# First two blocks of four sequence pairs moved to the front, and the weight pieces re-placed, in a windowed-attention and MLP kernel

## The chip, the cores and the metric

The kernel runs on one core of a Trainium2 chip. The metric is the device time of one execution in microseconds (us). TensorE is called PE below, ScalarE ACT, VectorE DVE, GpSimd POOL and SyncE SP.

## The reference

Eight sequences of 576 tokens, eight heads of 64, in float32. Attention with a causal window of 128 tokens and a linear distance bias, then a layer norm, a two-layer MLP (512 to 2048 to 512) and a residual:

```python
scores = scale * np.matmul(q, k.transpose(0, 1, 3, 2))
rel = pos[:, None] - pos[None, :]
bias = slopes[:, None, None] * (-np.abs(rel))[None, :, :]
mask = (rel >= 0) & (rel < window)          # window = 128
scores = np.where(mask, scores + bias[None], -1e9)
attn = softmax(scores); x = np.matmul(attn, v)   # laid out as [B, S, 512]
xn = (x - mu) / np.sqrt(var + 1e-06) * g_ln
out = x + np.maximum(xn @ w_ch1, 0.0) @ w_ch2
```

## The kernel before, in words

The 8 x 576 tokens are 36 blocks of 128. Two sequences make a pair of nine blocks; block 4 of a pair holds the end of one sequence and the start of the next. Within its pair a block has a number r from 0 to 8. A block with r = 0 looks only at itself, every other one also at the block before it.

Each block goes through `attention(i)` (L545): q and k are brought in, cast to 16 bits and turned so that the head dimension lies on partitions (`qkt`); then bias matmuls Z (L741; only in the first BY_BIAS blocks, later ones multiply with a mask table on DVE instead, L780), score matmuls S (L725), an exponential on ACT (L773), probability-value matmuls pv (L797), normalisation on DVE (L814, L818), centring xs (L858) and a transpose of xs on PE (TX, L872) whose copy is xt. Chunks of 3, 2, 3 and then 4 blocks go through `mlp(c)` (L907): layer 1, 16 groups of four matmuls (L919) with a relu on ACT or DVE, and layer 2 (L947) with the residual on DVE (L955). The eight weight pieces w0 to w7 (four of each layer, 1 MB in float32 each) are cast while POOL's DMA queue brings them in (L536, L538).

There are three ways for q and k. In a *span*, SP loads two neighbouring blocks as token pairs (`load_span`, L455: 512-byte packets, tiles `qs` and `ks`), one cast on POOL, DVE or ACT interleaves them (L619, L621), and PE turns both blocks together as 32-bit pairs (L639). A single block below LOAD_CAST comes by SP in 256-byte packets (`load`, L359), is cast (L560) and turned on PE (L687). From LOAD_CAST on, POOL's queue casts on the way (L473), and from QK_BY_DMA on a DMA transpose turns the block. The v of the first five blocks comes by SP and is cast to `vx` on ACT or POOL (L591, L593); later v comes by POOL's queue. Block 4 of the first pair is a single block in halves: six transfers of 64 partitions.

All of this is recorded as tasks. A planner (`Plan.run`, L103) plays them through with a cost for each engine, deadlines (`av`), hand-set shifts (PRI, HOLD) and lists of engines allowed for a cast or copy (PICK); it models DMA queues with rates (L96). The order in which it starts tasks is then written out for each engine (L988), with idle matmuls on a zero tile (L986) where PE has nothing to do in the first WARM microseconds of the plan. Waits on the chip come only from data and buffers: a dependency that exists in the plan alone, such as "weight piece n after the v cast of block i" (`weights`, L528, with W_AFTER, L525), orders instructions only where both stand on the same engine.

```python
    W_AFTER = [6, 12, 17, 18, 21, 22, 22, 28]
...
        if i in span_of:
            weights(i, (third,) * 3)
```

An entry of W_AFTER is three times a block's place plus 0, 1 or 2 for its q, k or v; in a span block all three stand for the v (`third`, L600).

Of the kernel before, what the change touches and what calls it, by code (L numbers as in the profile page):

```python
# [26 lines left out]
class Ring:  # L27
    def __init__(self, tiles):
        self.tiles, self.first, self.readers = tiles, {}, {}

    def __getitem__(self, k):
        return self.tiles[k % len(self.tiles)]
# [7 lines left out]
    def link(self):  # L40
        n = len(self.tiles)
        for k, tasks in self.first.items():
            for t in tasks:
                t.deps += self.readers.get(k - n, [])


class Plan:
# [8 lines left out]
    LANDING = {"DMA SP": (0.7, 1.3), "DMA ACT": (0.7, 1.3), "DMA POOL": (2.1, 1.4)}  # L56
    LAST_OF_RUN = 1.0
# [6 lines left out]
    def ring(self, tiles):  # L64
        r = Ring(tiles)
        self.rings.append(r)
        return r
# [28 lines left out]
    def rates(self, queues):  # L96
        on = [q for q, x in queues.items() if x]
        if "DMA POOL" in on and len(on) > 1:
            a, b = (0.92, 0.17) if len(queues["DMA POOL"]) > 1 else (0.7, 0.4)
            return {q: a if q == "DMA POOL" else b / (len(on) - 1) for q in on}  # L100
        return {q: 1.0 / len(on) for q in on}
# [125 lines left out]
def kernel(  # L227
# [10 lines left out]
    nc = tc.nc  # L238
# [30 lines left out]
    WARM = 22.0  # L269
    TABLE_AFTER = 4  # L270
    STATS_LEAD = 10.0
    MIX_AFTER = 4
    SPLIT = 4
    LOAD_CAST = 9
    V_CAST = 5
    BY_HALVES = [0, 2, 5]
    HALVED = []
    SPANS = [0, 2, 5, 7]
    SLACK = (0, 0.2, 0)
    PICK = {('xt', 0): 'ACT', ('xt', 8): 'ACT DVE', ('cv', 5): 'ACT', ('cv', 0): 'POOL', ('ev', 8): 'ACT', ('ev', 1): 'DVE ACT', ('ev', 3): 'ACT', ('ck', 8): 'ACT', ('cq', 5): 'ACT', ('ev', 5): 'DVE', ('ck', 2): 'POOL', ('ck', 7): 'POOL ACT', ('cq', 6): 'POOL', ('cq', 2): 'POOL ACT', ('xt', 6): 'ACT', ('cq', 8): 'POOL', ('xt', 5): 'ACT', ('cv', 7): 'POOL ACT', ('cv', 3): 'ACT', ('xt', 3): 'DVE', ('ev00', 4): 'ACT', ('cs1', 1): 'POOL ACT', ('cs0', 0): 'POOL DVE', ('ev10', 3): 'ACT', ('xt', 2): 'DVE', ('cq', 3): 'POOL', ('cs0', 8): 'ACT', ('ev01', 8): 'DVE ACT', ('ev10', 8): 'DVE ACT', ('ev11', 5): 'ACT', ('cs0', 2): 'DVE', ('cq', 4): 'POOL', ('ev00', 8): 'DVE', ('ev01', 0): 'DVE ACT', ('cv', 8): 'POOL ACT', ('ev11', 0): 'ACT', ('cv', 4): 'POOL ACT', ('ev01', 6): 'ACT', ('cv', 6): 'POOL ACT', ('ev10', 5): 'ACT', ('cs1', 4): 'POOL', ('ev', 0): 'DVE', ('cv', 2): 'POOL ACT', ('ev00', 2): 'DVE ACT', ('ev00', 7): 'ACT', ('ev10', 2): 'ACT', ('xt', 1): 'ACT DVE', ('ev11', 8): 'DVE', ('xt', 4): 'DVE', ('ev00', 1): 'DVE ACT', ('cv', 1): 'POOL ACT', ('ev01', 7): 'DVE ACT', ('ev11', 6): 'DVE ACT', ('cq', 1): 'ACT', ('ev01', 4): 'DVE', ('cs0', 5): 'POOL', ('ev', 7): 'ACT', ('xt', 7): 'ACT DVE', ('ev', 9): 'ACT', ('cv', 9): 'POOL', ('cq', 11): 'POOL ACT', ('cs1', 9): 'POOL ACT', ('ev00', 10): 'ACT', ('eva', 5): 'ACT', ('cka', 9): 'ACT', ('cv', 11): 'POOL ACT', ('cqa', 10): 'DVE', ('ckb', 10): 'ACT', ('ck', 10): 'ACT', ('ev00', 5): 'ACT', ('ckb', 3): 'DVE', ('evb', 5): 'DVE', ('ev', 11): 'DVE', ('ev01', 2): 'DVE ACT', ('ckb', 6): 'ACT', ('eva', 11): 'DVE', ('cqb', 7): 'POOL DVE ACT', ('cka', 1): 'POOL DVE ACT', ('ev00', 3): 'ACT', ('cq', 0): 'ACT', ('ev01', 5): 'DVE', ('cqb', 5): 'DVE', ('ev10', 4): 'DVE ACT', ('ev01', 9): 'ACT', ('cqa', 8): 'ACT', ('ev10', 10): 'DVE', ('evb', 4): 'DVE ACT', ('cqb', 8): 'POOL ACT', ('cs0', 9): 'POOL DVE', ('cka', 3): 'POOL', ('cqa', 2): 'DVE', ('cka', 8): 'ACT', ('cqa', 5): 'POOL DVE ACT', ('cq', 7): 'POOL', ('ck', 1): 'POOL', ('cka', 0): 'POOL ACT', ('cqa', 7): 'ACT', ('ev10', 11): 'ACT', ('cqa', 4): 'ACT', ('ev11', 11): 'DVE', ('eva', 10): 'DVE ACT', ('ev11', 4): 'DVE', ('eva', 3): 'DVE', ('ev11', 2): 'DVE', ('cqa', 6): 'POOL', ('cqa', 9): 'POOL ACT', ('cqa', 11): 'POOL DVE ACT', ('ev', 2): 'DVE ACT', ('cs0', 4): 'POOL ACT', ('ckb', 11): 'DVE', ('ckb', 2): 'POOL DVE ACT', ('ck', 5): 'POOL', ('cs1', 8): 'ACT', ('ev01', 10): 'DVE ACT', ('ev', 10): 'DVE ACT', ('cq', 10): 'POOL', ('eva', 4): 'DVE', ('cv', 10): 'POOL', ('ev', 6): 'DVE ACT', ('ck', 11): 'ACT', ('cs1', 11): 'POOL ACT', ('cqb', 1): 'DVE', ('ckb', 7): 'DVE', ('ev11', 1): 'DVE ACT', ('ck', 4): 'POOL ACT', ('cka', 11): 'DVE', ('ckb', 0): 'POOL ACT', ('cs1', 0): 'POOL DVE', ('eva', 7): 'DVE', ('cs0', 11): 'POOL ACT', ('evb', 8): 'DVE ACT', ('ev10', 6): 'DVE', ('eva', 2): 'DVE', ('cqb', 2): 'ACT', ('cq', 9): 'POOL ACT', ('ev10', 9): 'DVE ACT', ('ev10', 0): 'DVE ACT', ('evb', 6): 'DVE ACT', ('eva', 8): 'ACT', ('cqa', 3): 'POOL ACT', ('ck', 9): 'ACT', ('evb', 3): 'DVE ACT', ('cs0', 1): 'DVE', ('cqb', 9): 'POOL DVE ACT', ('cqb', 0): 'POOL', ('evb', 2): 'ACT', ('evb', 1): 'ACT', ('cqb', 6): 'DVE', ('eva', 9): 'ACT', ('evb', 10): 'ACT', ('cqb', 11): 'DVE', ('cka', 10): 'POOL', ('ck', 6): 'POOL ACT', ('ckb', 1): 'POOL', ('ev10', 7): 'ACT', ('cs1', 7): 'ACT', ('ev01', 3): 'DVE', ('cs0', 7): 'POOL', ('cs0', 6): 'POOL DVE', ('cs1', 3): 'DVE', ('cka', 2): 'POOL ACT', ('cqa', 1): 'POOL ACT', ('ev01', 1): 'ACT', ('cs0', 10): 'POOL ACT', ('cka', 4): 'ACT', ('ev00', 6): 'DVE', ('xt', 10): 'DVE', ('cqb', 3): 'POOL DVE ACT', ('evb', 0): 'DVE ACT', ('ev00', 0): 'ACT', ('xt', 9): 'ACT', ('ev11', 7): 'DVE', ('cqb', 4): 'POOL DVE ACT', ('ev00', 9): 'DVE', ('ev00', 11): 'DVE ACT', ('ckb', 9): 'POOL ACT', ('ev11', 3): 'DVE ACT', ('ev01', 11): 'DVE', ('evb', 7): 'DVE ACT', ('ckb', 4): 'POOL ACT', ('ckb', 5): 'POOL ACT', ('cs1', 5): 'ACT', ('cs0', 3): 'POOL DVE', ('cka', 7): 'POOL', ('ev11', 9): 'DVE', ('cka', 5): 'ACT', ('cqb', 10): 'POOL', ('cs1', 6): 'POOL DVE', ('eva', 6): 'DVE', ('cs1', 10): 'POOL ACT', ('eva', 1): 'DVE', ('evb', 9): 'DVE ACT', ('ev10', 1): 'ACT', ('eva', 0): 'DVE', ('cka', 6): 'POOL ACT', ('ev11', 10): 'ACT', ('ev', 4): 'ACT', ('ck', 3): 'POOL ACT', ('cs00', 0): 'POOL ACT', ('cs10', 3): 'DVE', ('cs01', 10): 'ACT', ('cs11', 6): 'POOL', ('cs00', 9): 'POOL', ('cs01', 11): 'POOL', ('cs11', 9): 'ACT', ('cs00', 6): 'POOL DVE', ('cs11', 3): 'POOL DVE', ('cs01', 7): 'POOL', ('cs01', 8): 'POOL DVE', ('cs10', 11): 'POOL ACT', ('cs00', 8): 'DVE', ('cqa', 0): 'ACT', ('cs00', 2): 'POOL', ('cs01', 6): 'DVE', ('cs10', 4): 'DVE', ('cs10', 10): 'POOL ACT', ('cs00', 4): 'POOL', ('ck', 0): 'ACT', ('cs11', 5): 'DVE', ('cs11', 2): 'POOL', ('cs11', 8): 'DVE', ('cs01', 1): 'POOL', ('cs01', 4): 'POOL DVE', ('cs00', 1): 'POOL DVE', ('cs11', 0): 'POOL', ('ckb', 8): 'DVE', ('cs10', 9): 'POOL ACT', ('cs01', 9): 'POOL ACT', ('cs00', 10): 'POOL', ('cs01', 2): 'POOL', ('cs00', 5): 'POOL', ('cs11', 11): 'ACT', ('cs00', 3): 'POOL ACT', ('cs10', 1): 'ACT', ('cs01', 3): 'POOL', ('cs11', 1): 'DVE', ('cs11', 10): 'POOL DVE', ('cs11', 4): 'ACT', ('cs10', 6): 'POOL ACT', ('cs11', 7): 'ACT', ('cs10', 0): 'DVE', ('cs10', 5): 'ACT', ('cs10', 7): 'POOL'}  # L280
    PRI = {'T7.1': -4.2, 'A1.13': 6.1, 'rc0.8': -3.5, 'B4.0': 5.4}
    HOLD = {'mkb5': 43.12, 'v8.i': 46.02, 'nm0.7': 54.13, 'cT0.01': 7.07, 'cT5.10': 33.76, 'qs0.0.i': 1.25, 'g.i': 0.8, 'sid1': 4.85, 'mreg00': 28.48, 'z1': 31.56, 'r0.3': 28.11, 'r0.11': 36.69, 'rc1.8': 61.94}
    BY_BIAS = 5
    MASK_AT = 5
    QK_BY_DMA = 9
    X_BY_DMA = 12
# [7 lines left out]
    def ring(name, n, shape, dt):  # L294
        return plan.ring([sb(f"{name}{i}", shape, dt) for i in range(n)])
# [11 lines left out]
    w1sb = [sb(f"w1sb{m}", [P, NKB, CH], FP16) for m in range(CB)]  # L307
    w2sb = [sb(f"w2sb{m}", [P, CB, d_model], FP16) for m in range(CB)]

    q32 = ring("q32", 2, [P, H, D], FP32)  # L310
    k32 = ring("k32", 2, [P, H, D], FP32)
    v32 = ring("v32", min(5, V_CAST), [P, H, D], FP32)
    qk16 = ring("qk16", 6, [P, 2, d_model], FP16)
# [713 lines left out]
```

## Time and profile before

| | us |
|---|---|
| median of 8 runs | 320.68 (320.01 to 322.92) |
| the profiled execution's own time | 320.61 |
| its span, first to last instruction | 318.9 |
| PE busy | 310.0 |
| ACT, DVE, POOL busy | 164.9, 184.6, 98.7 |
| first layer-1 matmul starts | 26.27 |
| first layer-2 matmul starts | 47.45 |
| w0, w1, w2, w3 issued | 15.1, 18.5, 24.7, 27.4 |
| w0, w1, w2, w3 landed | 22.9, 28.3, 35.8, 41.9 |
| v of blocks 0, 1, 2, 3 landed | 8.4, 9.5, 14.3, 16.9 |

Times inside the profile count from the first instruction of the span. A line of the timeline gives start, duration, engine, source line, operation, what it writes and reads, and how often; the bracket is the idle time ahead of it and what ended it. Time to landing is from the issue of a DMA until its semaphore is complete. A line of the waits gives the sum in us, the count and the longest. In the DMA view a queue's line has its packets, the MB moved (counted on the written side, so a cast from float32 counts half), and the time its packets took as a share of 16 engines. q0 is POOL's queue, q1 SP's and ACT's.

### The profile page before, as it was taken

The numbers are of one execution on the slowest core, as the hardware profiler recorded it, in microseconds if no ns is written. First come the engines' busy times: TensorE is split into PE (matmuls) and PEld (weight loads), VectorE is DVE, ScalarE is ACT, GpSimd is POOL, SyncE is SP. The second block draws the span as 40 slices with busy tenths as digits, with TensorE's granted clock in tenths as the row PEclk, the third lists the DMA queues.
The fourth block names the chain that finished last, engine by engine and source line by source line (L and its number), as shares of the span: only waits on it lengthen the run. The fifth ranks groups of instructions, "written<-read, shape, count | busy, mean of one in ns | idle before, by whom it ended". The sixth has DMA issues, their size and how long they took to land.

```text
span 318.9 us, 6461 instructions
## 1 busy us (share of the span) xinstructions
PE 310.0 (97%) x2526; PEld 176.4 (55%) x2526; DVE 184.6 (58%) x511; ACT 164.9 (52%) x269; POOL 98.7 (31%) x131
## 2 busy tenths in 40 slices
PE   8969999999999999999999999999999999999995
PEld 6757876556655554555555545554555455445543
DVE  3478568874599648664866486548664866111012
ACT  3668885445656742474257525752575257305600
POOL 5727375673654246354433241001000000000000
PEclk9799999999999999999999999999999999999999
DMA  7999999999999999999999998628710221011011
GB/s 190 237 182 240 210 209 175 154 189 174 156 144 165 157 160 163 172 185 149 171 215 99 100 156 175 49 50 135 131 19 16 85 82 19 17 68 67 0 65 68
DMA packets 153906, 41.47 MB, mean 130 GB/s; under 512 B 138385, under 2 KB 148881, under 8 KB 153874
## 3 DMA queue, kind: packets, MB, share of 16 engines
q0 software_dynamic: 91232, 15.34, 67.9%
q1 hardware_dynamic: 62640, 25.70, 42.1%
q8 instruction: 20, 0.33, 0.4%
q14 instruction: 12, 0.10, 0.1%
q10 hardware_dynamic: 2, 0.00, 0.0%
HBM read 36.70 MB, written 9.44 MB: 145 GB/s over the span
## 4 chain that ended last, share of the span: by engine, by line
PE 86%; DMA 7%; SPq 4%; POOL 1%; issue 0%; DVE 0%
PE fb L947 39%; PE fb L919 36%; PE sc L725 5%; PE fb L797 5%; DMA w1sb<-in_moe_w_ch_dram 5%; SPq L364 3%; DMA k<-in_k_dram 2%; SPq L459 2%; PE fb L872 1%; PE fb L639 0%; PE sc L741 0%; POOL vx L473 0%; POOL qs L621 0%; POOL qk L560 0%; PE fb L687 0%
## 5 line engine op out<-in xcount | busy, mean ns | idle before, releaser
L919 PE MATMUL fb<-xt,w1sb 128*128 128x512 f16 (+2 forms) x640 | 135.7, 359 | 0.4 <-DMA w1sb<-in_moe_w_ch_dram 0.4
L947 PE MATMUL fb<-w2sb,ht 128*128 128x512 f16 (+2 forms) x592 | 135.7, 373 | 0.0
L931 ACT ACTIVATE ht<-fb 128x512 f16<-128x512 f32 (+2 forms) x145 | 80.9, 560 | 62.0 <-PE fb L919 60.8
L773 ACT ACTIVATE probs<-sc 128x1024 f16<-128x1024 f32 (+1 forms) x72 | 67.6, 973 | 56.0 <-PE sc L725 55.9
L919 PEld LDWEIGHTS <-w1sb 128*128 128x128 f16 x640 | 68.3, 114 | 47.2 <-DMA w1sb<-in_moe_w_ch_dram 0.7
L947 PEld LDWEIGHTS <-ht 128*128 128x128 f16 x592 | 54.2, 98 | 56.9
L955 DVE SCALAR_TENSOR_TENSOR ot<-fb,rstd,xb 128x512 f32<-128x512 f32 (+2 forms) x37 | 27.2, 735 | 53.9 <-PE fb L947 53.6
L473 POOL DMA_DIRECT2D vx<-in_v_dram x34 | 28.8, 848 | 69.9 <-PE fb L797 57.6
L780 DVE TENSOR_TENSOR probs<-probs,mreg 128x1024 f16<-128x1024 f16 (+1 forms) x48 | 31.4, 656 | 28.7 <-ACT probs L773 28.4
L797 PEld LDWEIGHTS <-probs 128*128 128x128 f16 x544 | 25.5, 98 | 13.9
L818 DVE SCALAR_TENSOR_TENSOR xb<-fb,rec 128x256 f16<-128x256 f32 x72 | 30.4, 423 | 2.0
L473 POOL DMA_DIRECT2D qk<-in_q_dram x30 | 25.4, 846 | 19.7 <-DMA qkt<-qk 6.7
L473 POOL DMA_DIRECT2D qk<-in_k_dram x30 | 25.3, 844 | 13.6 <-DMA vx<-in_v_dram 6.2
L797 PE MATMUL fb<-vx,probs 128*128 128x65 f16 x544 | 28.6, 194 | 0.0
L858 DVE SCALAR_TENSOR_TENSOR xs<-xb,mean,g_t 128x512 f16<-128x512 f16 x36 | 26.9, 748 | 0.7
L839 DVE BATCH_NORM_STATS2 st<-xb 128x6 f32<-128x512 f16 x36 | 24.5, 683 | 0.0
L814 DVE RECIPROCAL rec<-fb 128x4 f32<-128x4 f32 x72 | 12.9, 180 | 19.3 <-PE fb L797 18.6
L725 PEld LDWEIGHTS <-qkt 64*128 64x128 f16 x544 | 15.4, 94 | 12.5 <-issue 10.5
L725 PE MATMUL sc<-qkt 64*128 64x128 f16 x288 | 19.8, 217 | 0.0
L725 PE MATMUL sc<-qkt,qkt 64*128 64x128 f16 x256 | 18.5, 219 | 0.0
L929 DVE TENSOR_SCALAR ht<-fb 128x384 f16<-128x384 f32 (+2 forms) x15 | 8.5, 565 | 5.2 <-PE fb L919 4.3
L650 ACT ACTIVATE qkt<-fb 128x512 f16<-128x512 f16 x10 | 5.7, 599 | 7.0 <-PE fb L639 6.4
(62 smaller groups left out, 124.5 us busy)
## 6 DMA issues: line engine op xcount, KB each, us to landing
out_dram<-ot SPq DMA_DIRECT2D x35, 256.0 KB, 3.5
vx<-in_v_dram POOLq DMA_DIRECT2D x28, 128.0 KB, 9.9
qk<-in_q_dram POOLq DMA_DIRECT2D x24, 128.0 KB, 11.0
qk<-in_k_dram POOLq DMA_DIRECT2D x24, 128.0 KB, 11.2
w1sb<-in_moe_w_ch_dram POOLq DMA_DIRECT2D x4, 512.0 KB, 10.5
w2sb<-in_moe_w_ch_dram POOLq DMA_DIRECT2D x4, 512.0 KB, 12.9
ks<-in_k_dram SPq DMA_DIRECT2D x6, 256.0 KB, 4.8
qs<-in_q_dram SPq DMA_DIRECT2D x6, 256.0 KB, 4.8
```

Source lines behind the costliest of these rows:

```text
L473: nc.gpsimd.dma_start(out=dst(p0, n), in_=src[b, :, s0 : s0 + n, :].rearrange("h p d -> p h d"))
L725: nc.tensor.matmul(scs[half][:, g, c0 : c0 + P], kt[rows, 1, hp, :], qkt[i][rows, 0, hp, :], start=not bias, stop=True, skip_group_check=True,
L773: nc.scalar.activation(out=o, in_=n_, func=AF.Exp, scale=inv_sqrt_d)
L780: en.tensor_tensor(out=pv, in0=pv, in1=mask[:, 2 * half : 2 * half + 2, :, lo:], op=ALU.mult)
L797: nc.tensor.matmul(pp[:, hh * (D + 1) : hh * (D + 1) + D + 1], probs[i][:, bank, slot, side * P : side * P + P], vx[i - 1 + side][:, h, 0 ...
L818: nc.vector.scalar_tensor_tensor(out=xb[i][:, 256 * half : 256 * half + 256].rearrange("p (h d) -> p h d", d=D), in0=pp[:, :, 0:D], scalar ...
L839: nc.vector.bn_stats(out=st[i][:, :], in_=xb[i][:, :])
L858: nc.vector.scalar_tensor_tensor(out=xs[i][:, :], in0=xb[i][:, :], scalar=mean[i][:, 0:1], in1=g_t[:, :], op0=ALU.subtract, op1=ALU.mult,)
L919: nc.tensor.matmul(fb[b][:, 0:n_], w1f[f // CB][:, kb, f % CB, :], xt[c][:, kb, 0:n_], start=(kb == 0), stop=(kb == NKB - 1),)
L931: nc.scalar.activation(out=ht[c][:, f, 0:n_], in_=src, func=AF.Relu)
L947: nc.tensor.matmul(pm[:, 0 : c1 - c0], ht[c][:, f, j * P : j * P + P], w2sb[f // CB][:, f % CB, c0:c1], start=(f == 0), stop=(f == NFB - 1),)
L955: nc.vector.scalar_tensor_tensor(out=ot[i][:, c0:c1], in0=fb[plan.held[key][1]][:, 0 : c1 - c0], scalar=rstd[c][:, j : j + 1], in1=xb[i][: ...
```

## The change

The order of the blocks is changed: places 0 to 7 hold blocks 0 and 1 of all four pairs, and the other 28 blocks follow in their old order (BLOCK). Everything that asked for block i - 1 now asks for the place of the neighbour before (`before`), the second block of each of the four pairs gets its own `vx` and `qkt` buffers that stay until its successor has been worked on (FAR, pinned tiles of a Ring), and the output rows follow BLOCK. The mixed block 4 of the first pair is thus no longer among the early ones. All eight early blocks are loaded as spans (SPANS), so q and k of all of them come as token pairs, only the first span in halves (before: the first, second and third). POOL's casting loads of q and k start with place 8. BY_BIAS and MASK_AT become 6, QK_BY_DMA 10, X_BY_DMA 10. W_AFTER moves the weight pieces. The planner's DMA rates become a table by weight or not and by the packet size of the other queue (SHARES), some of its costs, its slack, PRI and HOLD are new, and 178 entries of PICK differ or are new; among them, the v casts of places 2 and 3 may now only run on ACT, that of place 4 only on POOL.

```diff
+    SHARES = {
+        (True, 512): (0.83, 0.28), (True, 256): (0.75, 0.2), (True, 2048): (0.7, 0.4),
+        (False, 512): (0.38, 0.62), (False, 256): (0.5, 0.5), (False, 2048): (0.5, 0.5),
+    }
...
-            a, b = (0.92, 0.17) if len(queues["DMA POOL"]) > 1 else (0.7, 0.4)
+            others = [queues[q][0][0].name for q in on if q != "DMA POOL"]
+            size = 512 if any(n[:2] in ("qs", "ks") for n in others) else 256 if any(n[0] in "qkv" for n in others) else 2048
+            weight = queues["DMA POOL"][0][0].name[0] == "w"
+            a, b = self.SHARES[weight, size]
...
-    WARM = 22.0
-    TABLE_AFTER = 4
+    WARM = 20.0
+    TABLE_AFTER = 0
...
-    MIX_AFTER = 4
+    MIX_AFTER = 7
...
-    LOAD_CAST = 9
+    LOAD_CAST = 8
...
-    BY_HALVES = [0, 2, 5]
+    BY_HALVES = [0, 5]
...
-    SPANS = [0, 2, 5, 7]
-    SLACK = (0, 0.2, 0)
+    SPANS = [0, 2, 4, 6]
+    SLACK = (0, 1.3, 0.5)
...
-    BY_BIAS = 5
-    MASK_AT = 5
-    QK_BY_DMA = 9
-    X_BY_DMA = 12
+    HEADS = 4
+    BY_BIAS = 6
+    MASK_AT = 6
+    QK_BY_DMA = 10
+    X_BY_DMA = 10
...
+    BLOCK = [b for n in range(HEADS) for b in (PERIOD * n, PERIOD * n + 1)]
+    BLOCK += [b for b in range(NBLK) if b not in BLOCK]
+    PLACE = {b: i for i, b in enumerate(BLOCK)}
+    FAR = [i for i, b in enumerate(BLOCK) if b + 1 < NBLK and (b + 1) % PERIOD and PLACE[b + 1] > i + 1]
...
-    v32 = ring("v32", min(5, V_CAST), [P, H, D], FP32)
-    qk16 = ring("qk16", 6, [P, 2, d_model], FP16)
-    vx = ring("vx", 7 if V_CAST > 4 else 9, [P, H, VD], FP16)
-    qkt = ring("qkt", 6, [P, 2, HP, P], FP16)
+    v32 = ring("v32", min(4, V_CAST), [P, H, D], FP32)
+    qk16 = ring("qk16", 5, [P, 2, d_model], FP16)
+    vx = ring("vx", 7 if V_CAST > 4 else 9, [P, H, VD], FP16, FAR)
+    qkt = ring("qkt", 6, [P, 2, HP, P], FP16, FAR)
...
-    W_AFTER = [6, 12, 17, 18, 21, 22, 22, 28]
+    W_AFTER = [11, 12, 15, 17, 22, 22, 23, 23]
...
-        r = i % PERIOD
+        r = BLOCK[i] % PERIOD
+        before = PLACE[BLOCK[i] - 1] if r else None
...
-                                kt = qkt[i - 1 + side]
+                                kt = qkt[i if side else before]
...
-                    nc.sync.dma_start(out=out_flat[i * P : i * P + P, c0:c1], in_=ot[i][:, c0:c1])
+                    nc.sync.dma_start(out=out_flat[BLOCK[i] * P : BLOCK[i] * P + P, c0:c1], in_=ot[i][:, c0:c1])
```

In the order as built, POOL has first the cast of a half of k of the first span, then the v cast of place 1, then the issue of w0, the v cast of place 4, the issue of w1, v of place 5, the cast of q of the fourth span, the issues of w2 and w3, v of places 6 and 7, and w4 to w7. SP has the four half-span loads, v of places 0 and 1, q and k of the second span, v of 2 and 3, q and k of the third span, v of 4, q and k of the fourth span. ACT has, after the exponentials of places 0 and 1: the cast of k of the second span, an x copy, the v cast of place 2, an evacuation, the v cast of place 3, a mask row, the exponentials of place 2, the cast of q of the third span, a mask row, the exponentials of place 3, an evacuation, an x copy, an evacuation, a mask row, the logarithm of the first chunk's variances, the exponentials of place 4 with the rstd between them. PE has 92 idle matmuls in place of 76.

## The prediction

> **What bounds the kernel now.** I read the page's engine shares first, then the waits, then TensorE's timeline up to 60 us, then the DMA view by stretches, and last the ScalarE timeline.
>
> ```profile
> PE 310.0 (97%) x2526; PEld 176.4 (55%) x2526; DVE 184.6 (58%) x511; ACT 164.9 (52%) x269; POOL 98.7 (31%) x131
> PE fb L687 <- POOL qk L560: 2.5, 1, 2.5
> PE fb L639 <- POOL qs L621: 1.1, 1, 1.1
> PE fb L919 <- DMA w1sb<-in_moe_w_ch_dram: 0.4, 1, 0.4
> ```
>
> TensorE (PE) is busy 97% of the span, and its waits sum to under 6 us. So the time is PE's own work plus what PE loses early. The order of instructions gives the work: counts by shape, times start-to-start durations of the timeline (512-column matmul 0.216, 384: 0.162, 256: 0.108; 16 score matmuls 0.55; 8 probability-value matmuls 0.25; four 32-bit transposes 0.43; four 16-bit ones 0.22). That makes 296.0 us before and 296.0 us after. PE's last matmul ends near 315.5, so 19.5 us are lost, and only those can change.
>
> ```profile
> 21.02 0.39 PE L687 MATMUL fb<-iden,qk 128*128 128x128 f16 x4
> 23.94 0.40 PE L687 MATMUL fb<-iden,qk 128*128 128x128 f16 x4 [2.53 <-POOL qk L560]
> ...
> 26.27 0.84 PE L919 MATMUL fb<-xt,w1sb 128*128 128x384 f16 x4
> ...
> 41.91 2.14 PE L919 MATMUL fb<-xt,w1sb 128*128 128x384 f16 x12 [0.40 <-DMA w1sb<-in_moe_w_ch_dram]
> ...
> 47.45 1.03 PE L947 MATMUL fb<-w2sb,ht 128*128 128x512 f16 x4
> ```
>
> Where the loss stands: ahead of the first layer-1 matmul (26.27) lies 12.1 us of work, so 14.2 us are lost by then, in start-up, 76 filler matmuls and waits. Ahead of the first layer-2 matmul (47.45) lies 31.45 us: 16.0 lost. Of these 1.8 us more, 0.46 and 0.40 are waits; 0.9 is switching between kinds of matmul. The remaining 3.5 us trickle in by switching until the end. So the early stage is a race of data against PE work, settled by about 30 us.
>
> ```profile
> q1 hardware_dynamic: 1572, 0.39, 115.4%
> ```
> ```profile
> q0 software_dynamic: 422, 0.43, 85.5%
> q1 hardware_dynamic: 439, 0.11, 27.6%
> ```
>
> The first fence is the DMA view of 13 to 15 us: SP's queue (q1) alone moves 0.39 MB of 256-byte packets in 2 us, 0.195 MB/us. The second is 18 to 21 us, with the first weight piece (w0) flowing on POOL's queue (q0): SP gets 0.11 MB in 3 us, 0.037 MB/us, a fifth. w0 itself reads 0.29 MB/us (0.43 MB is the halved fp16 side). With 512-byte packets alone (9 to 11 us) SP moves 0.293 MB/us.
>
> ```profile
> 14.35 0.84 POOL L593 CAST vx<-v 128x512 f16<-128x512 f32 x1 [0.43 <-DMA v<-in_v_dram]
> 15.14 0.93 POOL L536 DMA_DIRECT2D w1sb<-in_moe_w_ch_dram  x1
> ```
>
> w0 is issued the moment POOL has done the v cast ahead of it, and lands 7.8 us later, in full flow from 2.9 to 6.4 us after issue.
>
> ```profile
> 17.06 0.62 ACT L650 ACTIVATE qkt<-fb 128x512 f16<-128x512 f16 x1
> 17.54 0.65 ACT L591 ACTIVATE vx<-v 128x512 f16<-128x512 f32 x1
> 18.46 1.94 ACT L773 ACTIVATE probs<-sc 128x1024 f16<-128x1024 f32 x2 [0.28 <-PE sc L725]
> ```
>
> ScalarE (ACT) rows: an evacuation takes 0.5 from its start to the next one's, a v cast 0.55, a pair of long exponentials 1.94. Today ACT reaches such a cast with the data there.
>
> [...] 0.037 to 0.29 MB/us is 1 to 8, as 256 to 2048 bytes. [...] The trace shows a dip: 0.59 from 8 to 10 us and 0.55 from 10 to 12, around a wait of 1.07 us; yet none followed the 2.5 us wait at 21.4.
>
> **The change part by part.**
>
> *PE's total.* Sequence-first blocks and bias matmuls: 32 wide bias matmuls become 24 wide and 16 more narrow ones (0.0 net), one more block is transposed on PE (+0.44), two fewer x transposes (-0.44). Sum 0. The X_BY_DMA transposes go to SP's queue after 50 us, where PE has 8 us of work per block and a DMA transpose lands in 4.5 to 8.5: nothing.
>
> *Fillers.* 92 instead of 76. They run where PE would idle; PE waits for data long after them. Nothing, unless PE runs late inside that stretch.
>
> *First data.* The first six SP transfers keep their order but for a swap: v1 lands at 9.5 (issue 3.5 + 6.0) as now. The next two are now 512 KB each instead of four halves: same bytes, both landed by 13.1. Gone is block 4's mixed load (six half-partition transfers, 0.79 MB) and the 2.5 us wait on it; the next spans and weights take its place.
>
> *w0 goes earlier, not later.* W_AFTER puts it behind block 3's v cast in the plan only; that cast is on ACT, and the built order shows no semaphore there. POOL now does: k cast, v1 cast, w0. So w0 issues at 9.5 + 0.62 = 10.2 instead of 15.1, and flows fully from 13.1 to 16.6. v2 is through by 13.0 and lands at 14.3. v3 (0.262 MB of 256-byte packets) meets w0: 3.5 us at 0.037 give 0.13 MB, the rest at 0.195 takes 0.7: data done 17.2, landed 18.3 (data to landing is 1.1 for v2); without w0 15.6. Then qs2 0.524 MB at 0.293: 19.0, landed 20.1; ks2 landed 21.9; v4 landed 23.3.
>
> *Who waits.* ACT's order is: v2 cast, one evacuation, the v3 cast, then everything else: block 2's exponentials stand behind v3. From 18.3, start to start by the present rows: v3 cast 0.55, mask row 0.32, two short exponentials 1.0 (20.2; qs2 is just there), qs2's cast 1.3 (two halves of 0.78, less overlap), mask 0.32, block 3's two exponentials 1.84, evacuation, x copy, evacuation 1.5, mask 0.32, log 0.3, block 4's exponentials with the rstd between 1.3. Sum 8.75: 27.05, with 0.15 for semaphores 27.2. PE then has in order: half of block 4's values 0.12, block 5's bias 0.87, a transpose 0.3, its scores 0.55. First layer-1 matmul: 29.1 us.
>
> *Sum.* Ahead of it stand 12.7 us: 16.4 lost. To the first layer-2 matmul add the same switching, 0.9, and some 0.2 for block 4's transpose, whose centred x on DVE is ready near 31.1. Lost 17.5 against 16.0: **+1.5 us**. Weights wait for nothing more: w1 follows v4's cast on POOL (23.9) and lands near 31.7, needed at 33.5; w2, behind qs3's cast (issue near 27), lands near 36, needed near 39; w3 39, needed 42; w4 to w7 have 7 us and more, since each takes 2.5. Unknown costs: a whole-span cast on ACT (not in the trace) lies between 1.2 and 1.6; v3's landing between 16.9 (v3's today, with only w0's first packets beside it) and 19.
>
> The span of 318.9 becomes 320.4, the profiled execution's 320.61 becomes 322.1; the median of the runs is 0.07 above that one: **322.2**.
>
> **Rivals.** *Cold clock* (slower still): by the span-2 transposes PE has 8.5 us of work and about 8 of fillers for 22 us, so it idles 5 or more, mostly from 16 on. One half-rate window of 3.4 us over the chain or the first layer-1 matmuls costs up to 1.7: 323.9. For it: the dip at 8 us. Against: none after 21.4. *Par*: ACT's casts are nearer the short ends and some exponentials fit in gaps: 0.5 to 1 us less, 321.4. *The other side*: w0 does not starve SP[...]. It decides where v3 lands before about 16.5. At 15.6 the same ACT chain ends at 24.4, layer 1 starts at 26.3, 13.6 lost, with 1.1 more 14.7 against 16.0: -1.3, 319.4. For it: no mixed load, fewer small packets; against: the 0.037 MB/us. *A weight piece late* (w1 or w2 at the 11 to 14.5 us that w2 and w3 take today): w1 at 35 adds 1.5, on top: 323.7 to 325.4.
>
> **How the numbers follow.** A measurement here can tell about 0.3% (1 us) from no change: faster is below 319.7, slower above 321.6. Forecast case (321.6 to 323.2) 0.40; cold clock or a late weight (to 325.4) 0.22; beyond that 0.07; par 0.18; the other side 0.13. So slower 0.69, same 0.18, faster 0.13. The range of 319.3 to 325.4 leaves out 0.07 above and some 0.1 below; the forecast's own range is 321.6 to 323.2.
>
> **What would show it.** In the new trace: w0 issued near 10.2; v3 landing near 18 and ACT's v cast waiting for it; block 4's second exponential ending near 27; first layer-1 matmul near 29; no wait for weights later. I am wrong if v3 lands by 16, if layer 1 starts before 27, or if PE waits again after 33 us.

## The result, and the profile after

The changed kernel takes 323.50 us (median of 12 runs, 321.42 to 325.50), the kernel before 320.61 (33 runs beside it): a ratio of 1.0089, 95% interval 1.0069 to 1.0108. It is slower, by 2.9 us; 322.2 was forecast. The profiled execution has a span of 320.4 us and an own time of 322.52, where 320.4 and 322.1 were forecast. So the profile fits the forecast closely and the median lies 1 us above the profile, which was not forecast. Six more runs, taken later (c1 below), have a median of 322.87; with them and the profiled execution there are 19 runs, and their median is 322.99.

Below, "block n" of the changed kernel is the block in place n.

The page of the changed kernel, its busy times and the granted clock over 40 slices of 8 us:

```profile
PE 311.5 (97%) x2550; PEld 177.7 (55%) x2550; DVE 188.3 (59%) x520; ACT 164.7 (51%) x266; POOL 93.9 (29%) x125
...
PEclk9979999999999999999999999999999999999999
```

PE is as busy as before. The third slice of the clock row, 16 to 24 us, shows 0.7. The waits of PE in the changed kernel (sum, count, longest):

```profile
PE fb L822 <- ACT probs L798: 3.9, 3, 2.8
...
```

The 2.5 us wait for POOL's cast of the mixed block is gone. A longer one is there instead, for ACT's exponentials. PE's timeline shows where:

```profile
19.89 0.30 PE L822 MATMUL fb<-vx,probs 128*128 128x65 f16 x4 [2.83 <-ACT probs L798]
...
27.32 0.30 PE L822 MATMUL fb<-vx,probs 128*128 128x65 f16 x4 [0.78 <-ACT probs L798]
27.89 0.30 PE L822 MATMUL fb<-vx,probs 128*128 128x65 f16 x4 [0.28 <-ACT probs L798]
...
29.78 1.49 PE L944 MATMUL fb<-xt,w1sb 128*128 128x384 f16 x8
...
51.12 2.75 PE L972 MATMUL fb<-w2sb,ht 128*128 128x512 f16 x12
```

Block 2's values wait 2.83 us, block 4's some 1.1. Layer 1 begins at 29.78 with 12.7 us of work ahead of it, so 17.1 us are lost by then (14.2 before). Layer 2 begins at 51.12 with 33.60 ahead: 17.5 lost (16.0 before). From there to the last matmul no more is lost than before, some 3.5 us in both kernels. ACT's timeline says what the exponentials stood behind:

```profile
15.36 0.58 ACT L677 ACTIVATE qkt<-fb 128x512 f16<-128x512 f16 x1
18.41 0.63 ACT L618 ACTIVATE vxp<-v 128x512 f16<-128x512 f32 x1 [2.47 <-DMA v<-in_v_dram]
...
19.25 1.06 ACT L798 ACTIVATE probs<-sc 128x512 f16<-128x512 f32 x2
20.21 1.34 ACT L646 ACTIVATE qs<-qs 128x1024 f16<-128x1024 f32 x1
...
22.63 1.94 ACT L798 ACTIVATE probs<-sc 128x1024 f16<-128x1024 f32 x2 [0.82 <-PE sc L750]
...
27.24 0.60 ACT L798 ACTIVATE probs<-sc 128x512 f16<-128x512 f32 x1
```

ACT stands at the v cast of block 3 (v3) for 2.47 us, for data that lands only at 18.4. Block 2's exponentials (19.25), whose scores PE had issued by 16.33, stand behind it in ACT's order. A second wait, 0.82 us for block 3's scores, was not forecast. POOL's timeline has the reason for the late data:

```profile
9.52 0.62 POOL L620 CAST vxp<-v 128x512 f16<-128x512 f32 x1 [1.47 <-DMA v<-in_v_dram]
10.08 0.93 POOL L562 DMA_DIRECT2D w1sb<-in_moe_w_ch_dram  x1
23.14 0.77 POOL L620 CAST vx<-v 128x512 f16<-128x512 f32 x1 [12.13 <-DMA v<-in_v_dram]
23.85 0.75 POOL L562 DMA_DIRECT2D w1sb<-in_moe_w_ch_dram  x1
```

The first weight piece (w0) is issued at 10.08 instead of 15.1. The view by stretches (length; busy time and count of PE, PEld, DVE, ACT and POOL; granted clock; DMA share; GB/s) shows what the 0.82 comes from:

```profile
18.00:20.00 2.00, 0.11 (x4) 0.12 (x5) 0.00 (x0) 1.59 (x4) 0.00 (x0) 1.00 1.19 292
20.00:22.00 2.00, 2.00 (x18) 1.26 (x18) 1.41 (x8) 1.81 (x3) 0.00 (x0) 0.55 1.23 246
22.00:24.00 2.00, 2.00 (x29) 1.80 (x30) 2.00 (x4) 1.37 (x2) 0.86 (x2) 0.60 1.08 276
```

After PE had stood nearly still, its clock was halved from 20.19 to 23.61, and block 3's bias and scores ran at half speed in there. In e1 below, where they ran at full speed (clock 1.00), ACT did not wait for them.

### The profile page after: what moved, and what is told of

Read it like the earlier page. It is cut to its first block, busy times and chain, and to the rows that moved or that the text cites. A ratio compares the mean times of both kernels' runs of the same rounds, so it can differ in the third digit from the quotient of the medians.

```text
span 320.4 us, 6509 instructions
## 1 busy us (share of the span) xinstructions
PE 311.5 (97%) x2550; PEld 177.7 (55%) x2550; DVE 188.3 (59%) x520; ACT 164.7 (51%) x266; POOL 93.9 (29%) x125
## 4 chain that ended last, share of the span: by engine, by line
PE 91%; DMA 3%; SPq 2%; ACT 1%; DVE 1%; issue 0%
PE fb L944 39%; PE fb L972 39%; PE sc L750 6%; PE fb L822 5%; DMA v<-in_v_dram 3%; SPq L483 1%; SPq L386 1%; PE sc L766 1%; PE fb L897 1%; PE fb L666 1%; ACT probs L798 0%; PE fb L1011 0%; PE fb L714 0%; DVE mmix L469 0%; ACT vxp L618 0%
## 5 line engine op out<-in xcount | busy, mean ns | idle before, releaser
L944 PE MATMUL fb<-xt,w1sb 128*128 128x512 f16 (+2 forms) x640 | 133.8, 359 | 0.0
L972 PE MATMUL fb<-w2sb,ht 128*128 128x512 f16 (+2 forms) x592 | 133.3, 373 | 0.2 <-DVE xb L843 0.2
L499 POOL DMA_DIRECT2D qk<-in_q_dram x32 | 27.6, 863 | 37.0 <-DMA qkt<-qk 26.1
L805 DVE TENSOR_TENSOR probs<-probs,mreg 128x1024 f16<-128x1024 f16 (+1 forms) x44 | 28.9, 673 | 13.3 <-ACT probs L798 13.3
L843 DVE SCALAR_TENSOR_TENSOR xb<-fb,rec 128x256 f16<-128x256 f32 x72 | 30.3, 422 | 1.9
L822 PE MATMUL fb<-vx,probs 128*128 128x65 f16 x480 | 27.0, 194 | 4.0 <-ACT probs L798 3.9
L499 POOL DMA_DIRECT2D qk<-in_k_dram x32 | 27.1, 851 | 2.8 <-DMA w2sb<-in_moe_w_ch_dram 2.1
L750 PEld LDWEIGHTS <-qkt 64*128 64x128 f16 x480 | 14.8, 95 | 11.3 <-issue 9.0
L750 PE MATMUL sc<-qkt 64*128 64x128 f16 x256 | 17.3, 216 | 0.1
L750 PE MATMUL sc<-qkt,qkt 64*128 64x128 f16 x192 | 13.5, 219 | 0.0
L954 DVE TENSOR_SCALAR ht<-fb 128x384 f16<-128x384 f32 (+2 forms) x17 | 9.9, 581 | 3.5 <-PE fb L944 3.3
L1011 PE MATMUL fb<-warm_t 128*128 128x128 f16 x92 | 8.9, 255 | 1.1 <-DVE warm_t L400 1.1
```

What stands on the lines that cost most here:

```text
L499: nc.gpsimd.dma_start(out=dst(p0, n), in_=src[b, :, s0 : s0 + n, :].rearrange("h p d -> p h d"))
L750: nc.tensor.matmul(scs[half][:, g, c0 : c0 + P], kt[rows, 1, hp, :], qkt[i][rows, 0, hp, :], start=not bias, stop=True, skip_group_check=True,
L805: en.tensor_tensor(out=pv, in0=pv, in1=mask[:, 2 * half : 2 * half + 2, :, lo:], op=ALU.mult)
L822: nc.tensor.matmul(pp[:, hh * (D + 1) : hh * (D + 1) + D + 1], probs[i][:, bank, slot, side * P : side * P + P], vx[i if side else before] ...
L843: nc.vector.scalar_tensor_tensor(out=xb[i][:, 256 * half : 256 * half + 256].rearrange("p (h d) -> p h d", d=D), in0=pp[:, :, 0:D], scalar ...
L944: nc.tensor.matmul(fb[b][:, 0:n_], w1f[f // CB][:, kb, f % CB, :], xt[c][:, kb, 0:n_], start=(kb == 0), stop=(kb == NKB - 1),)
```

## The experiments

The theory to be tested: w0 is issued too early, its large packets starve the small ones of v3, and ACT waits for v3 in order. The rivals: the bytes are the limit, whoever sends them (A); a weight piece that comes later is missed (B); what costs is the slow clock that PE's idling brings (cold clock). Each kernel below is the changed kernel with the edit shown. In the code, `order` is the list that the planner wrote, and lines of the source move by a few where lines were added.

One table first, from the profiled executions. "v3 cast" is the start of that cast, which stands for the landing of v3 here, as the traces have no landing for that transfer; "half clock" is when the clock record shows half speed (in e5 and e8 it shows full speed before 14.1 us, but PE's matmuls ran at half speed until about then: four 256-column bias matmuls took 1.06 us, against 0.60 in e1); layer 1 and layer 2 are the starts of their first matmuls; the last column is the median of all runs.

| kernel | w0 issued | v3 cast | half clock | layer 1 | layer 2 | own time | median (runs) |
|---|---|---|---|---|---|---|---|
| changed kernel | 10.1 | 18.41 | 20.2-23.6 | 29.78 | 51.12 | 322.52 | 323.50 (12) |
| c1, the same again | 10.1 | 18.86 | 8.0-11.4, 21.6-25.0 | 30.27 | 51.62 | 322.99 | 322.87 (6) |
| e1, w0 behind v3 | 16.5 | 16.30 | none | 26.48 | 48.08 | 319.18 | 319.32 (5) |
| e2, v3 cast on POOL | 9.8 | 18.82 | 21.5-28.3 | 30.01 | 51.57 | 322.76 | 323.50 (6) |
| e3, 42 fillers | 10.6 | 19.91 | 8.8-12.2 | 30.91 | 52.25 | 324.03 | 323.17 (6) |
| e4, v3 cast, then w0 | 16.3 | 15.71 | 8.0-14.8 | 28.14 | 49.63 | 320.91 | 319.44 (22) |
| e5, 61 fillers | 10.0 | 18.87 | to 14.1 | 31.29 | 52.63 | 324.35 | 322.02 (18) |
| e6, w0 in quarters | 10.0 | 17.41 | 18.8-22.2 | 29.57 | 50.91 | 322.49 | 322.58 (7) |
| e7, e1 with few fillers | 16.9 | 16.73 | 19.4-22.8 | 28.11 | 49.68 | 321.20 | 320.26 (22) |
| e8, w0 behind v4 | 21.6 | 18.49 | to 14.1 | 28.68 | 50.03 | 321.42 | 321.07 (14) |
| e9, e1 with 12 more fillers | 16.8 | 16.63 | none | 26.81 | 48.70 | 319.96 | 319.72 (13) |

In e5 and e8 ACT came to the v3 cast late and found its data there; in e1 ACT and the data came together; everywhere else in the table the data decided.

In all eleven, the own time less the start of layer 2 is 271.1 to 271.8. So all but 0.7 us of what differs between these executions is settled by the start of layer 2. In the changed kernel, e3, e4, e5 and e7 the profiled execution lies 0.9 to 2.3 us from the median, so the medians are compared, and the profiles are used for what they show inside.

**e1: w0 behind v3.**

```diff
+                if n == 0:
+                    nc.gpsimd.tensor_copy(out=peek[:, :], in_=v32[3][:, 0, 0:2])
                 if n < 4:
                     nc.gpsimd.dma_start(out=w1sb[m][:, :, :], ...)
```

> Ahead of the first weight piece (w0) GpSimd reads two elements of block 3's v, so w0 is issued when that v has landed; nothing else differs from the changed kernel. Theory (w0's large packets starve the small ones, and ScalarE waits in order for v3): v3 lands near 15.6 instead of 18.4, ScalarE's wait of 2.47 us shrinks below 0.5, w0 is issued near 16, the first layer-1 matmul starts at 26.3 to 27 instead of 29.8, the first layer-2 matmul has lost some 15 us instead of 17.5: 320.5 to 321.5 us, 2 to 3 less than the 323.5 of the changed kernel. Rival A (the bytes are the limit, whoever sends them): v3 still lands after 17.5, the time stays within 0.5 of 323.5. Rival B (weights late): w0 or w1 now comes too late, TensorE waits for weights after 26 us and the time is 323 or more.

319.32 us, ratio to the kernel before 0.9959 (0.9947 to 0.9971), 4.2 below the first measurement of the changed kernel (3.7 below the median of all its 19 runs) and 1.2 below the low end of what was expected. ACT, PE and POOL in e1:

```profile
16.30 0.63 ACT L621 ACTIVATE vxp<-v 128x512 f16<-128x512 f32 x1
...
19.60 1.93 ACT L801 ACTIVATE probs<-sc 128x1024 f16<-128x1024 f32 x2
...
23.91 0.64 ACT L801 ACTIVATE probs<-sc 128x512 f16<-128x512 f32 x1
```
```profile
17.78 0.30 PE L825 MATMUL fb<-vx,probs 128*128 128x65 f16 x4 [0.31 <-ACT probs L801]
...
26.48 1.49 PE L947 MATMUL fb<-xt,w1sb 128*128 128x384 f16 x8
...
48.08 11.57 PE L975 MATMUL fb<-w2sb,ht 128*128 128x512 f16 x52
```
```profile
16.34 0.19 POOL L563 COPY peek<-v 128x2 f32<-128x2 f32 x1 [6.07 <-DMA v<-in_v_dram]
16.46 0.93 POOL L565 DMA_DIRECT2D w1sb<-in_moe_w_ch_dram  x1
```

ACT's v3 cast has no wait left (its bracket is gone) and starts 2.1 us sooner; block 3's exponentials start 3.0 sooner, since the 0.82 is gone too; layer 1 starts 3.3 sooner, as expected. Holding back one instruction on POOL takes away more than the whole loss. w0, issued 6.4 us later, is not waited for, but only just: it lands at 26.22, 0.26 us before layer 1 begins. What e1 still differs in from the kernel before is the rest of the change, and that is a gain: -1.2 us. Rivals A and B, as they were stated, are out. Two things e1 can't tell. It takes the slow windows away with the late data (all five runs have a mean clock of 0.998 or more), so it doesn't divide the loss between them; e5 does. And w0 behind v3 takes both its bytes and its large packets out of v3's way; e6 parts these.

**e6: w0 early, but in small packets.**

```diff
-                    nc.gpsimd.dma_start(out=w1sb[m][:, :, :], in_=w1r[:, :, 512 * m : 512 * m + 512])
+                    s = 4 if n == 0 else 1
+                    for x in range(s):
+                        a, z = 512 * x // s, 512 * (x + 1) // s
+                        nc.gpsimd.dma_start(out=w1sb[m][:, :, a:z], in_=w1r[:, :, 512 * m + a : 512 * m + z])
```

> w0 stays early but is issued as four transfers of 128 columns, whose reads are 512-byte packets instead of 2048; the same bytes. Theory ([...] the share goes by packet size): the 256-byte packets of v get a third and not a ninth beside w0, v3 lands near 17 instead of 18.4 (read off ScalarE's v cast), w0 later than now but in time, the first layer-1 matmul at 28 to 28.8: 321.5 to 322.8 us. Rival A (a second queue takes its bytes whatever its packets are): v3 lands at 18.4 or later, 323.5 or more.

322.58 us. The DMA queues from 13 to 15 us (packets, MB, share of 16 engines; q0 is POOL's, q1 SP's with v2 and v3), first of the changed kernel, then of e1, then of e6:

```profile
q0 software_dynamic: 307, 0.31, 95.3%
q1 hardware_dynamic: 288, 0.07, 25.5%
```
```profile
q1 hardware_dynamic: 1313, 0.39, 104.2%
```
```profile
q0 software_dynamic: 639, 0.16, 82.3%
q1 hardware_dynamic: 1011, 0.25, 65.8%
```

With nothing beside it SP's queue moves 0.39 MB, beside w0's 2048-byte packets 0.07, beside the same w0 in 512-byte packets 0.25. The bytes are not the limit: in the changed kernel the two queues together read 0.70 MB in these 2 us (307 packets of 2048 bytes are 0.63), more than SP does alone. So rival A is out once more. POOL issues four transfers here instead of one, in 3.32 us instead of 0.93, but that is over by 13.3; from 13 to 16.6 us the time of POOL's packets makes 93.0% (82.0% in the changed kernel), and SP still moves 0.44 MB, against 0.25. So it is the size of w0's packets that takes SP's share. In the changed kernel the two queues make 307 and 288 packets from 13 to 15 us, about one for one. In e6 SP makes 1.6 packets for each of POOL's. So no fixed ratio of packets holds for both, and what sets it, no run here shows. But the gain in v3 did not come through. ACT and PE in e6:

```profile
17.41 0.63 ACT L621 ACTIVATE vxp<-v 128x512 f16<-128x512 f32 x1 [1.61 <-DMA v<-in_v_dram]
...
21.18 1.35 ACT L649 ACTIVATE qs<-qs 128x1024 f16<-128x1024 f32 x1 [1.86 <-DMA qs<-in_q_dram]
```
```profile
29.57 1.49 PE L947 MATMUL fb<-xt,w1sb 128*128 128x384 f16 x8
```

v3 is 1.0 us earlier, and the third span's q (qs2) 1.0 later (21.18 against 20.21): w0's bytes have to pass at some time, and here they stand beside qs2: from 16 to 18 us POOL's queue still makes 471 packets (46 in the changed kernel), and SP moves 0.42 MB instead of 0.55. The wait only moved, and layer 1 starts at 29.57, not at 28 to 28.8. The time came out inside the expected range, but it is only 0.4 below the 322.99 of the changed kernel, less than that kernel's two measurements differ by, so no gain is shown.

**e2: the same late data, but ACT is not the one that waits.**

```diff
+    move("cv3", "w0.i", engine="POOL", after=True)
```

> The cast of block 3's v moves from ScalarE to GpSimd, behind w0, which stays early: the data is as late, but ScalarE doesn't stand in front of it. Theory: block 2's exponentials run near 16.5 instead of 19.25, but the next thing in ScalarE's order, the cast of the third span's q, can't start before its data lands at 20.1: the wait only moves there, block 3's exponentials start near 21.7, and layer 1 near 29.0: 322.5 to 323.2 us, at most 1 less than the changed kernel. Rival A (the blocked ScalarE is the whole loss): layer 1 starts 2.5 earlier and the time is about 321. Rival C (cold clock): TensorE gets work at 17 to 19 and the slow clock window at 20 to 23.4 goes or moves; then up to 1 us less on top.

323.50 us, no gain, 0.3 above the expected range (six runs, from 321.88 to 324.78). ACT and PE in e2:

```profile
16.09 1.08 ACT L798 ACTIVATE probs<-sc 128x512 f16<-128x512 f32 x2
20.49 1.33 ACT L646 ACTIVATE qs<-qs 128x1024 f16<-128x1024 f32 x1 [3.32 <-DMA qs<-in_q_dram]
...
22.00 1.92 ACT L798 ACTIVATE probs<-sc 128x1024 f16<-128x1024 f32 x2
```
```profile
21.88 0.69 PE L666 MATMUL fb<-iden,qs 128*128 128x128 f32 x2 [2.50 <-ACT qs L646]
```

Block 2's exponentials run at 16.09, 3.2 earlier, as the theory said. Then ACT waits 3.32 us for qs2, which stands behind v3 in SP's queue, and PE waits 2.50 us at a new place. So v3 is only the first in a row of late data; all that SP loads behind it is late too. SP itself is held up: in the changed kernel it took 3.00 us to issue the third span's k, against 1.44 in e1, and what it issues next starts later. The slow clock did not go: in this profile it lasts two windows, 21.45 to 28.27, and block 3's exponentials (22.00) are 0.6 earlier while layer 1 is 0.2 later.

**e4: the planner's order made real.**

```diff
+    move("cv3", "w0.i", engine="POOL")
```

> The cast of block 3's v moves to GpSimd ahead of w0, so that w0 is issued behind it, as the planner's dependency had it. Theory: as the first experiment (v3 near 15.6, w0 near 16.4) and ScalarE is rid of 0.55 us more: 320 to 321.3 us, equal to the first experiment or up to 0.5 less. Rival A: within 0.5 of 323.5. Rival B (w0 or w1 late): TensorE waits for weights, 323 or more.

319.44 us, ratio to the kernel before 0.9967 (0.9956 to 0.9979), again below the range. It can't be told from e1; ACT's 0.55 us less gives nothing that can be measured. This is the remedy without a helper instruction: the change wanted w0 behind the v cast of block 3 and put that cast on an engine where it can't hold w0 back.

**e3 and e5: fillers, for the cold clock.**

```diff
+    FILL = {'pva2': 42}                              # e3
+    FILL = {'T0.1': 7, 'pva2': 44, 'T4.0': 10}       # e5
...
+            for _ in range(FILL.get(t.name, 0)):
+                nc.tensor.matmul(fb[3][:, 0:P], warm_t[:, :], warm_t[:, :], start=True, stop=True)
```

> 42 more filler matmuls run where TensorE idled for 2.83 us, ahead of block 2's probability-value product; nothing else differs from the changed kernel. Theory: the late data stays the bound; the slow clock window at 20 to 23.4 goes, which took 0.82 us (ScalarE's wait for block 3's scores) from the chain: 322.5 to 323 us, the first layer-1 matmul near 29.0. Rival C (the cold clock is what the change costs, and what spreads its runs): 321 or less, and the runs spread over less than half of the 4.1 us that they spread over now. Rival D (TensorE was never late in this stretch): no difference.

323.17 us, a little above the theory's range, over 6 runs that spread over 3.1: too little and too wide to decide. Its profile has no slow window at 20 us, which is what the fillers were for. It has one at 8.8 to 12.2 instead, and layer 1 is later, at 30.91. Not all of that is the clock: SP took 2.36 us to issue the second span's q (1.42 in the changed kernel), all later loads followed, and v3 came at 19.9. What held SP there stays open.

> The changed kernel with 61 more filler matmuls on TensorE, in all the places before 24 us where it idles: 7 ahead of block 0's second transposes (near 7 us), 44 ahead of block 2's probability-value product (near 17), 10 ahead of the third span's transposes (near 22). Data and casts are as late as in the changed kernel. The runs so far sort by the mean granted clock that each lists: of the changed kernel's 13, two at 0.998 or more took 321.5, four at 0.994 or 0.995 some 322.8, seven at 0.989 some 324.0. Theory (two costs: late data, and slow clock windows that the idle time brings): the windows go, most runs show 0.998 or more and take 321 to 322, and the median is there too, 1.5 to 2.5 below the changed kernel, yet 1 above the kernel before. Rival A (the windows are only a sign of a late start, no cost of their own): clock up, the median stays at 323 or more. Rival B (fillers don't govern the windows): most runs stay at 0.995 or lower.

322.02 us, ratio to the kernel before 1.0054 (1.0037 to 1.0070). All 18 runs have a mean clock of 0.998 or more, against 2 of 13 and 1 of 6 of the unaltered kernel (and 2 of 6 of e3), and the median falls by 1.5 from 323.50, by 1.0 from the 322.99 of all 19 runs. It is 1.5 above the kernel before, and its lowest run, 321.21, is still 0.7 above that kernel's median. So both rivals of this experiment are out, and so is the idea that the cold clock is all that the change costs: without slow windows it is still slower. Six of the 18 runs took 322.78 or more; the profiled one (324.35) shows a third thing, which the mean clock doesn't count. PE in it:

```profile
6.41 2.07 PE L439 MATMUL fb<-ot,ot 1*128 1x512 f32 x2
```

The matmul pair of L439 took 2.07 us, against 1.12 in c1 and in e1, and the 14 fillers from 3.82 on took 1.70, against 1.20 in e1; here PE ran at half speed until about 14.1 us. How many of the other runs began like this is not known.

**e7: the early data, few fillers.**

```diff
-                if t.start < WARM:
+                if t.start < 8.5:
```

(on top of e1)

> The first experiment (w0 behind v3) without the 61 filler matmuls after 8.5 us. Theory: the data comes as early as there, but TensorE is idle more, and slow clock windows come back: most runs at 0.995 or lower, each window some 0.5 to 1.3 us: 320 to 321.5. Rival: fillers after 8.5 us do nothing once the data is early: clock 0.998 or more in most runs, and 319.0 to 319.6.

320.26 us, against 319.32 of e1. 13 of its 22 runs have a clock of 0.995 or less; of the 40 runs of e1, e4 and e9 four have. In its profile ACT's v3 cast starts at 16.73, but PE's clock falls:

```profile
18.00:20.00 2.00, 1.80 (x28) 1.51 (x30) 1.39 (x8) 2.00 (x4) 0.00 (x0) 0.84 1.03 219
20.00:22.00 2.00, 2.00 (x17) 1.55 (x12) 1.86 (x4) 1.97 (x4) 0.00 (x0) 0.50 1.16 187
```

The slow window, 19.36 to 22.77, follows 3.41 us (15.95 to 19.36) in which PE was busy for 1.56, with a wait of 1.84. By the traces e7 leaves out 58 fillers (34 run, in e1 92; the expectation had counted 61). They compute nothing, and are worth 0.8 us here against the 319.5 of e1, e4 and e9 together, 0.9 against e1 alone. The rival is out.

**e9: both costs taken away.** (e1 and `FILL = {'T0.1': 7, 'pva2': 5}`)

> The first experiment (w0 behind v3) with 12 more filler matmuls: 7 near 7 us, 5 near 17. Both costs are taken away: data early and TensorE kept busy. Theory (two costs that add): the first layer-1 matmul at 26.3 to 26.8, hardly a run below 0.998, 318.8 to 319.5 us, some 1.2 below the kernel before and some 4 below the changed kernel. Rival (the first experiment's five runs were lucky in their clock): 319.8 or more.

319.72 us, ratio to the kernel before 0.9975 (0.9961 to 0.9990). 12 of 13 runs have 0.999 or more, yet it is not faster than e1 and 0.2 above what was expected: once the data is early, the fillers of the changed kernel seem to be enough. e1's five runs may have been a little lucky, but the intervals of e1 and e9 overlap; the 40 runs of e1, e4 and e9 together have a median of 319.5.

**e8: w0 still later.**

```diff
+    move("w0.i", "cv4", after=True)
```

> w0 still later: behind the cast of block 4's v on GpSimd, w1 right after it. Theory (w0 has room only until its own landing ends last): the casts come as early as in the first experiment or earlier, v4 lands near 19.5, w0 is issued near 20.3 and lands 7.8 later, near 28; the first layer-1 matmul waits for it and starts 1 to 2 us after the 26.5 of the first experiment: 320 to 321.5 us. Rival (the sooner the small packets are through, the better): 319.3 or less, no wait for w0.

321.07 us, inside the expected range, but the reason is not shown: in the profile PE ran at half speed until about 14.1 (the pair of L439 took 2.07 us here too), layer 1 starts at 28.68, and no wait for w0 is in front of it, which landed at 27.44, 1.2 us before. The runs fall in two groups, six at 319.95 to 320.55 and eight from 320.97 up; the lower one, 0.8 above e1, may be w0's lateness, the upper one the cold start. That is argued only. It does show that later than v3 isn't better.

**c1: the changed kernel again.**

> The changed kernel once more, unaltered, for a second profile and more runs by clock. Theory: 323 to 324 us; the runs at 0.998 or more near 321.5, those at 0.989 near 324; a profile at 0.989 has two slow windows of 3.41 us before 30 us, and its first layer-1 matmul starts later than 30.3. If windows cost nothing, the start of layer 1 is at 29.8 whatever the clock.

322.87 us, 0.6 below the first measurement. Its profile has two slow windows before 30 us, and layer 1 starts at 30.27, just short of the 30.3 expected and 0.5 after that of the first profile. With it and the profiled execution of the first measurement there are 19 runs of the changed kernel with a clock:

| mean clock | changed kernel: runs, median | kernel before: runs, median |
|---|---|---|
| 0.998 and more (no slow window) | 3, 321.57 | 32, 320.35 |
| 0.991 to 0.995 (about one) | 7, 322.76 | 61, 320.54 |
| 0.989 and less (two and more) | 9, 324.04 | 1, 322.82 |

One window of 3.41 us at half speed takes 0.5 x 3.41 / 320 = 0.0053 off the mean, so a step in the table is about one window. With each step the changed kernel takes 1.2 us more, the kernel before 0.2 (from none to one; it has a single run with two); and nine of 19 runs of the changed kernel have two, where the kernel before mostly has one or none. The table alone doesn't say that the window is the cause, since a late run may have its windows because it is late; e5, whose windows were taken away while the data stayed late, is what puts some 1.0 us on them.

## Why the prediction was right, and where it was not

*Slower, and by the mechanism named: right.* w0 issued at 10.1 (10.2 forecast), SP at 0.036 MB/us beside it (0.037), v3's cast at 18.41 (landing 18.3), qs2's cast at 20.21 (20.2), v4's at 23.14 (landing 23.3), w1 issued at 23.85 (23.9), no wait for a weight later. That ACT does not run past a cast that waits, on which the forecast rested, shows in the 2.47 us ahead of v3's cast, with block 2's exponentials run after it. e1 and e4 take away that one cause, each in its own way, and the loss is gone.

*The sizes of rows that the old trace didn't have: right.* The whole-span cast on ACT took 1.34 us (1.3 chosen between 1.2 and 1.6).

*ACT's chain of 8.75 us: 9.43.* From 18.41 to 27.84, when block 4's second exponential ended. The excess is the wait of 0.82 for block 3's scores, at half clock; without it the chain is 8.6, and in e1 8.25. The 0.15 for semaphores was an estimate; from the end of that exponential to PE's matmul (27.89) it was 0.05. The step that failed is the place of the cold clock in the working: it stood as a rival, a case of its own with a chance, while it comes on top of the late data in most runs (16 of 19 have a window).

*From layer 1 to layer 2, 1.1 us more lost: it was 0.44.* 0.9 for switching and 0.2 for DVE were too much. This hid the 0.7 by which layer 1 started later than forecast (29.78 against 29.1), and the profiled span came out at 320.4 to the tenth. Two terms missed in opposite directions: the agreement to the tenth is luck.

*The median 0.07 above the profiled execution: 1.0 in the 12 runs.* This is the term that was mis-sized. It was taken over from the kernel before, whose runs with and without a window differ by only 0.2. The profiled execution had one window, nine of 19 runs have two. But part of the 1.0 is chance: the median of all 19 runs is 0.5 above that execution, and in c1 it is 0.1 below the profiled one. So the forecast of 322.2 is 0.8 short of the 19 runs: 0.4 by this term, and 0.4 because the profiled own time is 2.1 us above its span here, 1.7 in the kernel before. A run without a window takes 321.57 (three runs) and so is 1.2 above a run of the kernel before without one, where the working without the clock said 1.5.

*"Fillers: nothing": too simple.* What 16 more of them do was not tested, but they are not without effect: e7 puts 0.8 to 0.9 us on 58 fewer, e5 1.0 to 1.5 on 61 more. The prediction had a sign of it, the dip at 8 us (clock 0.50 from 8.37 to 11.78 in the kernel before), and set it aside because none followed the 2.5 us wait at 21.4. The slow stretches in the traces are 3.41 or 6.83 us long and stand at other places in two profiles of the same kernel (20.19 in one, 7.96 and 21.61 in the other). Ahead of each of them PE had done some work: 0.58 us and more in the 3.41 us before. What decides whether one follows a wait, these traces don't show. One trace without a dip is no evidence that a wait is free.

*The other side, 319.4 if v3 lands by 16: its number was right for the kernel that has it.* e1 puts v3's cast at 16.3 and layer 1 at 26.48 (26.3 forecast), with 14.5 us lost by layer 2 (14.7), and takes 319.32. The change without w0's early issue is worth about 1.0 us (319.5 against some 320.5); which part of it does that, the new order of the blocks or another, was not tested. w0's early issue costs 3.5 us (322.99 against 319.5; 4.0 by the first measurement) and turns that round. Of the 3.5, about 2.5 is the late data itself, since e5, warm in all its runs by the mean clock, is that much above 319.5; about 1.0 is the slow clock that the late data brings.

What stays open: what held SP's issue in e3, why a slow start lasts until 14.1 us in some runs, and how e8's time divides.

## What to carry to other kernels

Here a dependency that existed only in the planner held nothing back on the chip: look in the built order at which engine issues a transfer and what really stands ahead of it there. In this kernel an early bulk transfer with large packets held back many small ones that were due sooner (SP's queue moved 0.07 MB in 2 us, against 0.39 with nothing beside it), and the loads behind these in their queue were late as well (a wait of 3.32 us for qs2 in e2), so that curing the first wait (e2) or giving it a larger share (e6) only moved the wait to the next load. And where a wait of some microseconds empties TensorE (2.83 us here, and 16 of 19 runs had a mean clock of 0.995 or less), forecast the median with the slow clock in it, and sort the runs by their clock before explaining their spread.

## What the runs showed of the hardware that was not expected

- A half-clock window of 3.41 us doesn't cost a fixed time: runs with one are 0.2 us longer than runs without in the kernel before, 1.2 in the changed one, 0.9 in e7, and no longer in e4 (three runs with one). What makes the difference, no run shows.
- The mean granted clock of a run doesn't count a slow start: two profiles at 0.998 (e5) and 1.0 (e8) ran PE at half speed until about 14.1 us (2.07 us for the matmul pair of L439, 1.12 in e1).
- Busy time alone doesn't say when the clock falls. In the five profiles with a slow window after 18 us (changed kernel, c1, e2, e6, e7) PE was busy for 0.58 to 1.58 of the 3.41 us ahead of it; in the kernel before, 22.02 to 25.43 had 1.49 and no window followed. Before 12 us a window followed stretches with 2.37 to 2.99 busy (kernel before, c1, e3, e4), and none followed stretches of 2.93 and 2.88 in e1.
- The time from issue to landing of the same weight piece is not fixed: w0 was issued anywhere from 9.8 to 21.6 us and took 5.9 (e8) to 9.8 us (e1) in one transfer. In the eleven profiles only e1 shows PE waiting for a weight at all, 0.3 us of its weight loads ahead of w1; w0's room was used up there, too.
